# DCN-v2 cross layers on one core: bias load first on ScalarE's queue, bias sums among the fillers, odd lanes' first tail weights on SyncE

## The chip, the cores and the metric

The kernel runs on one core of one Trainium2 chip. The metric is device time in microseconds (us) of one execution; lower is better. The kernel before takes 130.96 us, the median of three runs (130.64 to 131.13).

Times inside a kernel come from traces. They count from the start of the span, which ends with the last instruction and is some 1.9 us shorter than the time measured for the execution. Each trace is one execution. "Landing" is when the last of a load's completion updates arrives at its semaphore.

## The reference

```python
# x0 [4096, 416], ws [6, 416, 416], bs [6, 416], all bf16
def reference(x0, ws, bs):
    x = x0
    for l in range(ws.shape[0]):
        x = x0 * (x @ ws[l] + bs[l]) + x
    return x
```

## The kernel before

The activations are kept transposed: 416 features are three chunks of 128 on the partitions (`x0T_sb`, `xT_sb`) and a tail of 32. The 4096 rows are four superblocks of 1024, so there are 4 x 6 = 24 layer passes. Every matmul of the main part is split over four 32-column tiles of the array ("lanes"). The products of all layers are summed up in the same PSUM banks, since x behind layer l is x0 times (1 + the sum of x W + b over the layers up to l). So the biases are first turned into running sums too, by 16 tiny matmuls against a triangle (`bias_sums`), and these sums enter the layers as scalars.

The start-up matters here. Four queues of work begin at once:

```python
# SyncE's queue
sp.dma_start(xin_sb[:, 0:2, :], x0_v[:, 0:2, :])          # first rows, 208 KB
sp.dma_start(w_sb[:, 0, 0, :], ws[0, 0:128, :])           # first weights (chunk k=0), 104 KB
sp.dma_start(xin_sb[:, 4:6, :], x0_v[:, 4:6, :])          # third rows, 208 KB
sp.dma_start_transpose(x0T_sb[:, :, 768:SB], x0[768:SB, 0:DF])   # the transposing load
...                                                        # layer 1's weights and so on

# ScalarE's queue
act.dma_start(xin_sb[:, 2:4, :], x0_v[:, 2:4, :])         # second rows, 208 KB
act.dma_start(w_sb[:, 0, 1:NC, :], ...)                   # second weights (k=1 and k=2), 208 KB
act.dma_start(xtl_sb[:, :, :], x0_v[:, 6:JS, DF:D])       # tail rows, 16 KB
for g in (1, 3):
    load_wt(act, g, 0, 1, s_wt[0])                        # odd lanes' first tail weights

# GpSimd's queue
pool.memset(ones_sb[:, :], 1.0)
pool.dma_start(bsa_sb[1:L + 1, :], bs[:, :])              # biases, 4.9 KB, 6 rows
...                                                        # identity, triangle, even lanes' tail weights, corner weights
```

(semaphore updates cut). TensorE, meanwhile:

```python
fill(14)                              # 14 groups of four matmuls on constants, to no purpose but time and clock
pe.wait_ge(s_set, 1)                  # identity
for i, (h, c) in enumerate(IN_ORDER): # (0,0),(1,0),(0,1),(1,1),(0,2),(1,2): half h, chunk c
    if i in (0, 1):
        pe.wait_ge(s_xin[h], 16)      # first rows, second rows
    ...                               # two transposes
# first layer pass, first half, chunk by chunk of the contraction
pe.wait_ge(s_w0, 16)
for k in range(NC):
    if k == 1:
        pe.wait_ge(s_w[0], 16)        # second weights
    if k == 2:
        bias_sums()                   # 16 matmuls of six columns
        pe.wait_ge(s_xin[2], 16)      # third rows
        pe.wait_ge(s_xtl0, 16)        # tail rows
        tail_inputs()                 # small transposes of the tails ...
        third_input()                 # ... and of the third quarter
    before_a(k)                       # copies of the transposed chunk k by VectorE or ScalarE
    for m in range(NC):
        step(m, 0, k)                 # "main products" of chunk k
...                                   # then the "row part": tail features and corner weights
```

In these words: the first main products are k = 0 and k = 1, then the small transposes, then k = 2, then the row part. From there the 24 layer passes follow each other.

## Time and profile before

| Quantity (before) | Value | From |
|---|---|---|
| span of the profiled execution | 128.7 us | page |
| TensorE busy | 124.2 us, 97% | page, busy times |
| one layer pass | 4.87 us | chain |
| start of the row part | 8.22 us | TensorE's timeline |
| rest of the span behind it | 120.5 us | difference |
| second weights on ScalarE: issue, landing | 1.35, 5.24 us | trace |
| tail rows on ScalarE: issue, landing | 1.87, 6.17 us | trace |
| third rows on SyncE: issue, landing | 1.82, 5.80 us | trace |
| transposing load on SyncE: issue, landing | 2.29, 7.34 us | trace |

The table is read like this. TensorE is the bound, and everything behind the row part is 120.5 us. Each of the four loads has a place in TensorE's order, and each lands well before TensorE wants it: the second weights at about 5.9 us (3 of the 6 product groups after 5.29), third rows and tail rows at 6.89, the transposing load at 8.8.

### The profile page before, as it was taken

To read this page: it belongs to the slowest core of one execution; us is meant where nothing else is said; L and a number is where in the kernel's file an instruction comes from. 1 tells how busy PE (TensorE), PEld (TensorE's weight loads), DVE (VectorE), ACT (ScalarE), POOL (GpSimd) and SP (SyncE) were. 2 spreads that over 40 slices of the span, in tenths; PEclk is the share of its full clock that TensorE was granted. 3 is DMA by queue.
4 is the path that set the end of the run, shared out by engine and by line. 5 is a ranking of instruction groups with operands and counts; after the bars stand their busy time and mean duration, and the time that the engine had idled before them with its cause. 6 is when DMAs were issued, how large, how long until landed. Compare 5 with 4: busy or idle time off the path is not lost.

```text
span 128.7 us, 5404 instructions
## 1 busy us (share of the span) xinstructions
PE 124.2 (97%) x2448; PEld 62.6 (49%) x2448; DVE 100.1 (78%) x154; ACT 71.3 (55%) x163; POOL 23.1 (18%) x42
## 2 busy tenths in 40 slices
PE   7999999999999999999999999999999999999980
PEld 6654544444444444444445445445445445445450
DVE  2349779779779779779779779779779779789780
ACT  0637357377737357376736456476745555555670
POOL 7802202202202103102102013012012013022130
PEclk9999999999999999999999999999999999999998
DMA  3974399400008698700009996800009900700026
GB/s 109 298 162 104 89 255 174 116 0 5 3 8 167 130 128 185 256 5 0 5 0 175 103 183 140 270 0 0 5 0 95 180 0 0 265 5 5 0 83 190
DMA packets 32918, 12.54 MB, mean 97 GB/s; under 512 B 25338, under 2 KB 32896, under 8 KB 32896
## 3 DMA queue, kind: packets, MB, share of 16 engines
q1 hardware_dynamic: 31488, 11.47, 42.8%
q10 hardware_dynamic: 1184, 0.67, 1.8%
q8 instruction: 19, 0.31, 1.0%
q0 software_dynamic: 224, 0.06, 0.2%
q14 instruction: 3, 0.02, 0.1%
HBM read 2.90 MB, written 3.41 MB: 49 GB/s over the span
## 4 chain that ended last, share of the span: by engine, by line
PE 96%; DVE 1%; DVEq 0%; issue 0%
PE ps L212 84%; PE ps L351 10%; PE ps L250 1%; DVE xo_sb L459 1%; DVE o_sb L464 0%; DVEq L33 0%; PE ps L367 0%
## 5 line engine op out<-in xcount | busy, mean ns | idle before, releaser
L459 DVE SCALAR_TENSOR_TENSOR xT_sb<-ps,cb_sb,x0T_sb 128x512 bf16<-128x512 f32 x120 | 80.9, 744 | 16.5 <-PE ps L351 16.5
L212 PE MATMUL ps<-xT_sb,w_sb 128*32 128x512 bf16 (+1 forms) x1680 | 89.0, 364 | 0.0
L212 PEld LDWEIGHTS ps<-xT_sb,w_sb 128*32 128x32 bf16 x1680 | 43.0, 97 | 38.7 <-issue 4.2
L486 ACT ACTIVATE xt_sb<-xt_sb 32x256 bf16<-32x256 bf16 x80 | 33.1, 414 | 16.6 <-POOL xt_sb L199 15.9
L506 ACT ACTIVATE t_sb<-ps,cb_sb 64x256 f32<-64x256 f32 x48 | 22.5, 469 | 30.1 <-PE ps L212 29.8
L199 POOL TENSOR_TENSOR xt_sb<-t_sb,x0t_sb 128x256 bf16<-128x256 f32 x20 | 13.4, 671 | 83.4 <-ACT t_sb L506 83.4
L212 PE MATMUL ps<-x0T_sb,w_sb 128*32 128x512 bf16 (+1 forms) x336 | 18.5, 364 | 0.0
L459 DVE SCALAR_TENSOR_TENSOR xo_sb<-ps,cb_sb,x0T_sb 128x512 bf16<-128x512 f32 x23 | 15.6, 745 | 3.7 <-PE ps L351 3.3
L212 PEld LDWEIGHTS ps<-x0T_sb,w_sb 128*32 128x32 bf16 x336 | 8.5, 97 | 7.5 <-issue 0.8
L351 PE MATMUL ps<-xt_sb,wt_sb 32*128 32x512 bf16 x80 | 12.1, 379 | 0.0
L519 ACT ACTIVATE x0t_sb<-x_sb 32x256 bf16<-32x256 bf16 x24 | 9.9, 413 | 0.4
L367 PE MATMUL ps<-xt_sb,wt_sb 32*128 32x512 bf16 x40 | 7.8, 385 | 0.0
L351 PE MATMUL ps<-xt_sb,wc_sb 32*128 32x256 bf16 x80 | 7.7, 268 | 0.0
L351 PEld LDWEIGHTS ps<-xt_sb,wt_sb 32*128 32x128 bf16 x80 | 2.3, 92 | 8.5 <-DVE xT_sb L459 8.5
L351 PEld LDWEIGHTS ps<-xt_sb,wc_sb 32*128 32x128 bf16 x80 | 4.0, 93 | 2.3
L199 POOL TENSOR_TENSOR xot_sb<-t_sb,x0t_sb 128x256 bf16<-128x256 f32 x4 | 2.7, 672 | 12.6 <-ACT t_sb L506 12.6
L212 PE MATMUL ps<-const-bfloat16-1.0 128*32 128x256 bf16 x56 | 3.2, 419 | 0.8 <-PEq L557 0.8
L481 ACT ACT_TABLE_LOAD x1 | 1.3, 1283 | 3.6 <-issue 3.6
L432 DVE COPY x0T_sb<-ps 128x256 bf16<-128x256 bf16 x4 | 1.0, 288 | 2.9 <-PE ps L250 2.9
L212 PEld LDWEIGHTS ps<-const-bfloat16-1.0 128*32 128x32 bf16 x56 | 2.4, 144 | 1.2 <-issue 0.8
L351 PE MATMUL ps<-x0t_sb,wt_sb 32*128 32x512 bf16 x16 | 2.5, 380 | 0.0
L168 POOL DMA_DIRECT2D wc_sb<-in_ws_dram x4 | 2.2, 549 | 0.0
(44 smaller groups left out, 28.7 us busy)
## 6 DMA issues: line engine op xcount, KB each, us to landing
out_dram<-o_sb SPq DMA_DIRECT2D x3, 832.0 KB, 4.1
w_sb<-in_ws_dram SPq DMA_DIRECT2D x5, 312.0 KB, 3.9
xin_sb<-in_x_dram SPq DMA_DIRECT2D x2, 208.0 KB, 3.4
out_dram<-o_sb SPq DMA_DIRECT2D x1, 256.0 KB, 2.4
xin_sb<-in_x_dram ACTq DMA_DIRECT2D x1, 208.0 KB, 3.1
w_sb<-in_ws_dram ACTq DMA_DIRECT2D x1, 208.0 KB, 3.9
out_dram<-o_sb SPq DMA_DIRECT2D x1, 208.0 KB, 2.2
out_dram<-o_sb ACTq DMA_DIRECT2D x1, 208.0 KB, 2.7
```

The costliest lines, as they stand in the source:

```text
L168: pool.dma_start(wc_sb[lane(g), a:b, 32 * g:32 * g + 32], ws[a:b, DF:D, DF:D].rearrange("l p n -> p l n")).then_inc(s_wc[i], 16)
L199: pool.tensor_tensor(out=dst, in0=t32_sb[:, n % 2, :], in1=x0t_sb[:, s, 0:G], op=ALU.mult).then_inc(s_xt, 1)
L212: return pe.matmul(dst, lhsT=lhsT, rhs=rhs, start=start, stop=True, skip_group_check=True, tile_position=(0, 32 * q),)
L250: ins = pe.transpose(out=psT[:, IN_BANKS[h][c], (j % 2) * 128:(j % 2 + 1) * 128], in_=xin_sb[:, j, c * 128:(c + 1) * 128], identity=ident[ ...
L351: return pe.matmul(dst, lhsT=lhsT, rhs=srct[lane(g), cols], start=l == 0 and start, stop=True, skip_group_check=True, tile_position=(32 * ...
L367: pe.matmul(ps[:, NC * h + 2, :], lhsT=wt_sb[lane(g), l, 0:128], rhs=srct[lane(g), :].rearrange("p (b r) -> p b r", b=2)[:, ::-1, :], star ...
L432: dve.tensor_copy(out=x0T_sb[:, c, h * 256:(h + 1) * 256], in_=psT[:, IN_BANKS[h][c], 0:256]).then_inc(s_inD, 1)
L459: dve.scalar_tensor_tensor(out=dst, in0=ps[:, NC * half + c, :], scalar=cb_sb[:, c, l:l + 1], in1=x0T_sb[:, c, o:o + H], op0=ALU.add, op1= ...
L481: act.activation(out=x0T_sb[:, 1, h * 256:(h + 1) * 256], in_=psT[:, IN_BANKS[h][1], 0:256], func=ACTF.Copy).then_inc(s_inA, 1)
L486: ins = act.activation(out=buf[lane(g), G:2 * G], in_=buf[lane(g ^ 1), 0:G], func=ACTF.Copy)
L506: ins = act.activation(out=t32_sb[HALVES[h], n % 2, :], in_=tail(h), func=ACTF.Identity, bias=cb_sb[HALVES[h], NC, l:l + 1],)
L519: ins = act.activation(out=x0t_sb[lane(g), s + 1, swap * G:(swap + 1) * G], in_=x4_sb[96:128, s, r * G:(r + 1) * G], func=ACTF.Copy,)
```

## The change

The intent: the bias sums hold TensorE for about 0.3 us between the main products and the small transposes, when it has real work. Put them among the fillers, where TensorE only waits for input. For that the biases have to come sooner, so their load leaves GpSimd's queue and becomes the first on ScalarE's. To make room, the odd lanes' first tail weights leave ScalarE's queue for SyncE's, ahead of the transposing load. The transposes are reordered, first half entirely first, so that the second rows, now second on ScalarE's queue, are wanted later.

```diff
-        IN_ORDER = ((0, 0), (1, 0), (0, 1), (1, 1), (0, 2), (1, 2))
+        IN_ORDER = ((0, 0), (0, 1), (0, 2), (1, 0), (1, 1), (1, 2))
 # SyncE
             sp.dma_start(xin_sb[:, 4:6, :], x0_v[:, 4:6, :]).then_inc(s_xin[2], 16)
+            for g in (1, 3):
+                load_wt(sp, g, 0, 1, s_wt[0])
             sp.dma_start_transpose(x0T_sb[:, :, 768:SB], ...)
 # GpSimd
-            pool.dma_start(bsa_sb[1:L + 1, :], bs[:, :]).then_inc(s_bs, 16)
 # TensorE
-            fill(14)
+            fill(10)
+            bias_sums()
+            fill(2)
...
                             if k == 2:
-                                bias_sums()
                                 pe.wait_ge(s_xin[2], 16)
 # ScalarE
+            act.dma_start(bsa_sb[1:L + 1, :], bs[:, :]).then_inc(s_bs, 16)
             act.dma_start(xin_sb[:, 2:4, :], ...)
             act.dma_start(w_sb[:, 0, 1:NC, :], ...)
             act.dma_start(xtl_sb[:, :, :], ...)
-            for g in (1, 3):
-                load_wt(act, g, 0, 1, s_wt[0])
```

Cut here: the sums go to PSUM bank 1 instead of 4, VectorE copies them before its first input copy, the waits on that copy and on the input copies are renumbered for the new order.

More of the change, by code (lines that the diff above doesn't have):

```diff
@@ L242, in third_input, with bias_sums @@
                     ins.then_inc(s_inT, 1)
-            fill(14)
+            def bias_sums():
+                pe.wait_ge(s_bs, 16)
+                pe.wait_ge(s_zero, 2)
+                pe.wait_ge(s_set, 2)
+                for c in range(NC + 1):
+                    for q in range(4):
+                        f0 = c * 128 + 32 * q if c < NC else DF
+                        ins = tile_mm(ps[lane(q), 1, c * 8:c * 8 + L], bsa_sb[:, f0:f0 + 32], u_sb[:, :], q, True)
+                ins.then_inc(s_cbp, 1)
+            fill(10)
+            bias_sums()
+            fill(2)
             pe.wait_ge(s_set, 1)
             for i, (h, c) in enumerate(IN_ORDER):
-                if i in (0, 1):
+                if c == 0:
                     pe.wait_ge(s_xin[h], 16)
@@ L254, in _ @@
                 ins.then_inc(s_inT, 1)
-            def bias_sums():
-                pe.wait_ge(s_bs, 16)
-                pe.wait_ge(s_zero, 2)
-                pe.wait_ge(s_set, 2)
-                for c in range(NC + 1):
-                    for q in range(4):
-                        f0 = c * 128 + 32 * q if c < NC else DF
-                        ins = tile_mm(ps[lane(q), 4, c * 8:c * 8 + L], bsa_sb[:, f0:f0 + 32], u_sb[:, :], q, True)
-                ins.then_inc(s_cbp, 1)
             def out_chunk(c):
@@ L304, in before_a @@
                         if n == 0:
-                            pe.wait_ge((s_inD, s_inA, s_inD)[k], (2, 2, 4)[k])
+                            pe.wait_ge((s_inD, s_inA, s_inD)[k], (3, 2, 4)[k])
                         else:
@@ L323, in _ @@
                             for m in range(NC):
+                                if k == 0 and m == 1:
+                                    pe.wait_ge(s_cb, 1)
                                 step(m, 0, k)
@@ L334, in _ @@
                         pe.wait_ge(s_te, 1)
-                        pe.wait_ge(s_cb, 1)
                     else:
@@ L428, in _ @@
             dve.memset(bsa_sb[0:1, :], 1.0).then_inc(s_zero, 1)
+            dve.wait_ge(s_cbp, 1)
+            dve.tensor_copy(
+                out=cb_sb[:, :, :], in_=ps[:, 1, 0:8 * (NC + 1)].rearrange("p (c e) -> p c e", e=8)[:, :, 0:L],
+            ).then_inc(s_cb, 1)
             for i, (h, c) in enumerate(IN_ORDER):
@@ L434, in _ @@
                     ).then_inc(s_inD, 1)
-            dve.wait_ge(s_cbp, 1)
-            dve.tensor_copy(
-                out=cb_sb[:, :, :], in_=ps[:, 4, 0:8 * (NC + 1)].rearrange("p (c e) -> p c e", e=8)[:, :, 0:L],
-            ).then_inc(s_cb, 1)
             for c in (0, 2):
@@ L476, in _ @@
             act.dma_start(xtl_sb[:, :, :], x0_v[:, 6:JS, DF:D]).then_inc(s_xtl0, 16)
-            for g in (1, 3):
-                load_wt(act, g, 0, 1, s_wt[0])
             for h in range(2):
-                act.wait_ge(s_inT, h + 3)
+                act.wait_ge(s_inT, NC * h + 2)
                 act.activation(
```

## The prediction

> **What bounds the kernel now.** I read the chain that ended last first, then TensorE's timeline of the first ten microseconds, then the landings of the loads. The chain of the first 14 us (start us, length us, what) is TensorE without a break:
>
> ```profile
> 0.85 3.18 PE ps L212 x51
> 4.03 1.33 PE ps L250 x12
> 5.36 2.93 PE ps L212 x92
> 8.29 0.32 PE ps L351
> ...
> 8.62 0.26 PE ps L351 x4
> 8.88 4.33 PE ps L212 x84
> ```
>
> The page says the same of the whole run:
>
> ```profile
> PE 96%; DVE 1%; DVEq 0%; issue 0%
> ```
>
> The reader should see two things. From 8.88 us on, each layer is one block of 84 matmuls (4.33 us) and a row part; it returns every 4.87 us (8.88, 13.75, 18.62 ...), 24 times, with TensorE never short of input. No line of the change touches this part. Everything that the change can move lies before 8.88 us, and a microsecond counts there only if TensorE's instructions come earlier or later.
>
> TensorE's timeline of that start (start us, length us, shapes, count):
>
> ```profile
> 0.85 3.18 PE L212 MATMUL ps<-const-bfloat16-1.0 128*32 128x256 bf16 x56 [0.85 <-PEq L557]
> 3.96 1.40 PE L250 MATMUL ps<-ident,xin_sb 128*128 128x128 bf16 x12
> 5.29 1.48 PE L212 MATMUL ps<-x0T_sb,w_sb 128*32 128x512 bf16 x24
> 6.70 0.26 PE L212 MATMUL ps<-u_sb,bsa_sb 7*32 7x6 bf16 x16
> 6.89 0.24 PE L212 MATMUL ps<-ident,xin_sb 128*32 128x128 bf16 x3
> ...
> 7.46 0.83 PE L212 MATMUL ps<-x0T_sb,w_sb 128*32 128x512 bf16 x12
> 8.22 0.38 PE L351 MATMUL ps<-x0t_sb,wt_sb 32*128 32x512 bf16 x1
> ...
> 8.48 0.28 PE L351 MATMUL ps<-x0t_sb,wc_sb 32*128 32x256 bf16 x1
> ...
> 8.81 2.45 PE L212 MATMUL ps<-x0T_sb,w_sb 128*32 128x256 bf16 x48
> ```
>
> In order: 14 groups of four fillers; 12 input transposes; the main products for chunks 0 and 1 (24 matmuls, six groups of four); the bias sums; 40 small matmuls that transpose tails and the third quarter (6.89 to 7.46); chunk 2; the row part for the tails; the rest. The bias sums are 16 matmuls of six columns, yet they hold TensorE from about 6.60 (5.29 plus six groups at 0.22; the steady block gives 4.33 us / 19.5 groups of 512 columns = 0.22) to 6.89: **0.29 us**[...]. That is the prize.
>
> **What the skill says.** "TensorE: Matmul & The Clock Gate", section "What's actually happening": the array runs at half rate until it has been busy for a window of about 3.4 us. The trace agrees: a transpose of 128 columns costs 1.33/12 = 0.111 us at 4.0 to 5.3 us, while ten groups of 128 columns cost 0.57/10 = 0.057 us after 6.89. A filler group of 256 columns costs 3.18/14 = 0.227 us with the last one's drain; one filler lasts 0.419, twice 0.21, so without the drain it is (3.18 - 0.2)/14 = 0.213. So the fillers have two purposes: they bridge the wait for the first rows and they earn the full rate, which here arrives around the end of the transposes. "DMA: Bandwidth & Descriptors", section "Issuing engines are not separate DMA queues": loads from several engines share the same 16 DMA engines, and another issuer saves issue time alone. So I take a moved load to shift by issue times and by its place in its queue, not to get bandwidth; the trace has the DMA engines full between about 2 and 8 us (page: busy 9 tenths or more in the second slice, 3.2 to 6.4 us), in agreement. Same page, "Latency and other measured facts": the first byte comes some 0.6 us after issue from SyncE or ScalarE and about 1 us from GpSimd. The trace has no such split but the same order: 2.9 us to landing for the first SyncE load of 208 KB against 3.7 us for 4.9 KB of biases from GpSimd.
>
> **The change part by part.** Landings are issue start plus time to landing, from the view of each load's line.
>
> *Bias load from GpSimd to ScalarE.* Now it is issued at 1.38 and takes 3.7 us: 5.1 us, too late for the fillers.
>
> ```profile
> 1.38 0.72 POOL L165 DMA_DIRECT2D bsa_sb<-in_bs_dram  x1 [0.26 <-issue]
> ...
> 2.56 1.10 POOL L107 DMA_DIRECT2D wt_sb<-in_ws_dram  x2
> 3.67 2.17 POOL L168 DMA_DIRECT2D wc_sb<-in_ws_dram x4
> ```
>
> On ScalarE it is issued at 0.82. A large store at the end of this kernel, with quiet DMA engines, takes 2.2 us; I allow 2.2 to 2.5, an estimate, so it lands at 3.0 to 3.3. GpSimd's queue loses 0.72 us ahead of everything behind it: identity and triangle are ready near 1.9 instead of 2.6, and the first-layer corner weights, whose second load is issued at 4.16 and lands at about 8.4, land at about 7.65. That matters: the second half of the row part starts at 8.48, just behind that landing. Without this step an earlier row part would have been held there and most of the 0.29 us lost.
>
> *Bias sums among the fillers.* TensorE does 10 groups: 0.85 + 10 x 0.213 = 3.0 us. The biases land at 3.0 to 3.3, say 3.15, a wait of about 0.15. The sums cost 0.29 now; with the array at half rate I estimate 0.35. Two more filler groups, 0.43. First transpose: 3.0 + 0.15 + 0.35 + 0.43 = 3.95, against 3.96 now. The rows of the first half land at 0.81 + 2.9 = 3.7, so they don't hold it. Call this shift 0, give or take 0.2.
>
> *New order of the transposes.* Chunk 0 of the second half moves from places 3 and 4 to 7 and 8 of 12. VectorE now begins its first copy 0.43 us after the first transpose (4.39 against 3.96, two transposes in) and copies in 0.29. Six transposes later that becomes 0.43 + 0.64 + 0.29 = 1.36 us, and with about 0.06 for the semaphore the first main matmul comes 1.42 us after the first transpose instead of 1.33: **0.09 us lost**. In return the second rows, now behind the biases on ScalarE's queue (0.5 us per issue: 3.9 becomes about 4.4), are wanted only at 3.95 + 0.64 = 4.6. The wait for the constants' copy before block m=1 is over long before.
>
> *After the main products.* The small transposes follow at once, in the same tiling: **0.29 us saved**. Start: 3.95 + 1.42 + 1.31 = 6.68 instead of 6.89. The tail rows (now 1.87 + 4.3 = 6.2 us) go back by one ScalarE issue less what the queue hides: 6.2 to 6.7. This is the tightest load.
>
> *Odd tail weights on SyncE.* Two issues of about 0.45 us ahead of the transposing load put it from 2.29 to about 3.2; it takes 5.0 us, so 8.2 instead of 7.3. It is wanted at 8.81, in the new kernel at about 8.6: hidden, with 0.4 us to spare. The next weights (3.62 + 4.8 = 8.4, later 9.3) are wanted at 10.9: hidden. ScalarE saves 1.21 us of issues less 0.5 for the biases and loads its table (1.28 us at 3.63) some 0.7 us sooner, so its first copy never has to wait for it; that copy is not on the path.
>
> Sum: 0 (start) + 0.09 - 0.29 = **-0.20 us** on the row part and thus on all after it. With a little given back to the tail rows I predict -0.16: 130.96 - 0.16 = **130.8 us**, 0.1% faster.
>
> **Rivals.**
> *The biases land late.* Each tenth after 3.15 delays the fillers, the transposes and everything else by a tenth; at 3.4 to 3.5 the gain is gone (131.0), at 3.8, where the first 208 KB on this queue land today (0.82 + 3.1 = 3.9), the kernel is 0.4 slower (131.4). For it: the first loads of both queues land at 3.7 and 3.9. Against: those are 208 KB and this is 4.9 KB.
> *The clock.* A hole of 0.2 us and 16 tiny matmuls among the fillers could make the array count as idle for that window and let it run at half rate longer. Between 5.3 and 8.8 us TensorE has about 3.4 us of full-rate work, so a whole missed window would cost up to 1.7 us (132.5). For it: nothing measured, only that the fillers are thinner. Against: the hole is a twentieth of a window. I give it one chance in fifteen.
> *A load takes over the wait.* If the tail rows land near 6.7 or the transposing load near 8.6 TensorE stops there and the whole 0.2 us goes: 131.0.
> *Nothing hidden, better than thought.* If the biases land by 3.0 and the sums cost no more than 0.29 the first transpose comes at 3.75 and the gain is 0.4: 130.55.
>
> **Range and chances.** The three runs of before spread over 0.5 us (130.64 to 131.13), more than the predicted gain. The mechanisms span -0.4 to +0.4 apart from the clock. So 130.45 to 131.25. Two per cent is 2.6 us: no removable time before 8.88 us comes near that, and even a missed clock window stays below. Faster by 2%: 0.01; within: 0.975; slower: 0.015.
>
> **What would show it.** In the changed profile: bias matmuls at 3.0 to 3.3 us; first transpose at 3.8 to 4.1; first main matmul 1.4 us later; the small transposes directly behind the main products near 6.7, with no idle weight load before them; the row part near 8.05; then blocks every 4.87 us as before. I am wrong if TensorE is idle over 0.3 us before the bias sums, if the transposes or the first main groups still run at half rate past 5.5 us, if it waits for tail rows or the transposing load, or if the period of the layers changes.

## The result, and the profile after

The kernel after takes **131.70 us** (median of six runs, 131.51 to 132.28) against 130.78 us (median of six, 130.41 to 131.13) for the kernel before on the same chip in the same rounds. Executions over 1.5% slower than the fastest of the same kernel are left out of the means. The ratio is 1.008, with a 95% interval of 1.0052 to 1.0106. Ratios in this document are the mean time of one kernel's fast runs over that of the other's of the same rounds, so not quite the ratio of the medians that are quoted. So the kernel became 0.8% slower, about 1.0 us; 131.70 lies above the predicted range, which ended at 131.25.

The profiled execution of after has a span of 130.2 us, 1.5 us longer than that of before. The page's summary of the chain that ended last, after (shares of the span by engine):

```profile
PE 90%; DMA 5%; ACTq 1%; DVE 1%; issue 0%; DVEq 0%
```

Where TensorE had 96% of this chain, a DMA now has 5% and ScalarE's issues of DMAs 1%. The chain of the first 15 us of after, in order of time (start us, length us, what), names them:

```profile
0.81 0.58 ACTq L477
...
1.42 0.41 ACTq L478
...
1.86 0.48 ACTq L479
...
2.37 5.93 DMA xtl_sb<-in_x_dram
8.30 0.14 issue
8.43 1.40 PE ps L213 x52
9.83 0.32 PE ps L354
...
10.38 4.33 PE ps L213 x84
```

The start is no longer TensorE without a break. It is ScalarE's queue: bias load (L477), second rows (L478), second weights (L479), then the tail rows, which take 5.93 us for 16 KB. TensorE begins its small transposes at 8.43, behind their landing, and the first block of 84 starts at 10.38 instead of 8.88.

TensorE's timeline of after shows that there is a second wait ahead of that one (start us, length us, shapes, count; in brackets the idle time before it and what ended it):

```profile
0.85 2.32 PE L213 MATMUL ps<-const-bfloat16-1.0 128*32 128x256 bf16 x40 [0.85 <-PEq L559]
3.10 0.27 PE L213 MATMUL ps<-u_sb,bsa_sb 7*32 7x6 bf16 x16
3.30 0.62 PE L213 MATMUL ps<-const-bfloat16-1.0 128*32 128x256 bf16 x8
3.85 0.95 PE L263 MATMUL ps<-ident,xin_sb 128*128 128x128 bf16 x12
5.14 0.83 PE L213 MATMUL ps<-x0T_sb,w_sb 128*32 128x512 bf16 x12 [0.34 <-DVE x0T_sb L439]
7.28 0.83 PE L213 MATMUL ps<-x0T_sb,w_sb 128*32 128x512 bf16 x12 [1.30 <-DMA w_sb<-in_ws_dram]
8.43 0.24 PE L213 MATMUL ps<-ident,xin_sb 128*32 128x128 bf16 x3 [0.33 <-DMA xtl_sb<-in_x_dram]
...
8.99 0.84 PE L213 MATMUL ps<-x0T_sb,w_sb 128*32 128x512 bf16 x12
9.77 0.38 PE L354 MATMUL ps<-x0t_sb,wt_sb 32*128 32x512 bf16 x1
```

Read it down to 5.14 and, in this execution, the change works: the bias sums run among the fillers, the first transpose comes at 3.85 (before: 3.96), the first main product at 5.14 (before: 5.29). Then k = 1 waits for the second weights. The chain does not show this wait, since the tail rows, on the same queue behind those weights, ended later still; a chain names the last wait and not each.

The sum, from starts in the two timelines. A product of three groups takes 0.65 us (half of the 1.31 us that the prediction found for six), so k = 1 could have begun at 5.14 + 0.65 = 5.79 and began at 7.28: 1.49 lost. The small transposes could have begun at 7.28 + 0.65 = 7.93 and began at 8.43: 0.50 lost. The bias sums are gone from this place: 0.29 won. The first main product is 0.15 earlier. 1.49 + 0.50 - 0.29 - 0.15 = 1.55 us, and the row part moved from 8.22 to 9.77, which is 1.55 us. (The brackets say 1.30 and 0.33: they count idle time from the modelled end of the last matmul, which is later than where the next one could start.) The sum says where the time went, not what each load costs by itself: the tail rows landed at 8.30, so the small transposes would have begun near 8.43 even with the second weights on time. The tail rows' landing alone sets the 1.55 us.

Behind the row part nothing changed: 128.75 - 8.22 = 120.53 us in before, 130.23 - 9.77 = 120.46 us in after. The profiled execution of after (132.09 us) happened to be one of its longer ones; on average the loss is 1.0 us.

The loads' own views give the cause a size. Line of the second weights and of the tail rows, before (count; shortest/median/longest issue in ns, first and last issue time; then, as the last line of each load's answer, the time to landing):

```profile
L475 ACTq DMA_DIRECT2D w_sb<-in_ws_dram x1: 492/492/492, 1.3 to 1.3; - x1
...
DMA to landing us min/median/max: 3.9/3.9/3.9
L476 ACTq DMA_DIRECT2D xtl_sb<-in_x_dram x1: 491/491/491, 1.9 to 1.9; - x1
...
DMA to landing us min/median/max: 4.3/4.3/4.3
```

and after:

```profile
L479 ACTq DMA_DIRECT2D w_sb<-in_ws_dram x1: 481/481/481, 1.9 to 1.9; - x1
...
DMA to landing us min/median/max: 5.4/5.4/5.4
L480 ACTq DMA_DIRECT2D xtl_sb<-in_x_dram x1: 492/492/492, 2.4 to 2.4; - x1
...
DMA to landing us min/median/max: 5.9/5.9/5.9
```

Both are issued half a microsecond later, as expected. In before the second weights take 3.9 us from there and the tail rows 4.3 us; in after 5.4 and 5.9. All loads of the start, from the trace (issue → landing, us):

| Load | Queue, before | Before | Queue, after | After |
|---|---|---|---|---|
| first rows | SyncE | 0.81 → 3.68 | SyncE | 0.81 → 3.44 |
| first weights | SyncE | 1.32 → 4.22 | SyncE | 1.32 → 3.76 |
| third rows | SyncE | 1.82 → 5.80 | SyncE | 1.82 → 6.55 |
| transposing load | SyncE | 2.29 → 7.34 | SyncE | 3.26 → 9.27 |
| biases | GpSimd | 1.38 → 5.10 | ScalarE | 0.81 → 2.26 |
| second rows | ScalarE | 0.82 → 3.94 | ScalarE | 1.42 → 4.25 |
| **second weights** | ScalarE | 1.35 → 5.24 | ScalarE | 1.86 → **7.23** |
| **tail rows** | ScalarE | 1.87 → 6.17 | ScalarE | 2.37 → **8.30** |
| odd lanes' tail weights, last | ScalarE | 2.9 → 7.60 | SyncE | 2.80 → 8.24 |
| corner weights of layer 0, last | GpSimd | 4.16 → 8.34 | GpSimd | 3.29 → 8.67 |

For the second weights an issue 0.51 us later made a landing 1.99 us later. That factor of four is what the experiments are about.

A last view, the windows (stretch, its length, busy us and count of TensorE, its weight loads, VectorE, ScalarE, GpSimd; granted clock; DMA share; GB/s). Before:

```profile
5.00:6.25 1.25, 1.25 (x24) 0.68 (x26) 0.49 (x2) 0.59 (x2) 0.84 (x2) 1.00 1.28 256
5.75:6.75 1.00, 1.00 (x28) 0.36 (x23) 0.00 (x0) 0.00 (x0) 0.09 (x1) 1.00 1.18 258
```

After:

```profile
5.00:6.25 1.25, 0.83 (x12) 0.27 (x12) 0.20 (x1) 0.12 (x1) 0.00 (x0) 1.00 1.75 252
5.75:6.75 1.00, 0.22 (x7) 0.00 (x0) 0.00 (x0) 0.00 (x0) 0.00 (x0) 1.00 1.47 130
```

The reader should compare the last two columns. From 5.75 to 6.75 the packets of after fill the DMA engines' time more (share 1.47 against 1.18; above 1 means more than one packet of an engine is open at a time), yet half as many bytes move. The packet records of the trace show why: 17 packets of 256 bytes begin between 5.70 and 6.29 and all end near 6.92 (6.90 to 6.95). In before the longest packet that begins between 5.00 and 6.50 takes 0.28 us (0.44 from 4.25 on). I call them **standing packets**. They have the size of the transposing load's own packets: in before exactly 768 of 256 bytes begin on SyncE's queue by 6.3 us, which is its 256 rows times three chunks of 128 features.

### The profile page after: what moved, and what is told of

It is laid out like the page before. It is cut to its first block, busy times and chain, and to the rows that moved or that the text cites.

```text
span 130.2 us, 5388 instructions
## 1 busy us (share of the span) xinstructions
PE 123.8 (95%) x2440; PEld 61.6 (47%) x2440; DVE 100.0 (77%) x154; ACT 71.4 (55%) x163; POOL 22.6 (17%) x41
## 4 chain that ended last, share of the span: by engine, by line
PE 90%; DMA 5%; ACTq 1%; DVE 1%; issue 0%; DVEq 0%
PE ps L213 80%; PE ps L354 10%; DMA xtl_sb<-in_x_dram 5%; DVE xo_sb L462 1%; DVE o_sb L467 0%; ACTq L477 0%; ACTq L479 0%; ACTq L478 0%; DVEq L33 0%; PE ps L370 0%
## 5 line engine op out<-in xcount | busy, mean ns | idle before, releaser
L444 DVE CAST x0T_sb<-ps 128x256 bf16<-128x256 f32 x2 | 0.8, 420 | 3.8 <-PE ps L213 3.8
L492 ACT ACTIVATE x0t_sb<-ps 128x512 bf16<-128x512 f32 x1 | 0.6, 597 | 3.8 <-PE ps L213 3.8
L213 PEld LDWEIGHTS ps<-const-bfloat16-1.0 128*32 128x32 bf16 x48 | 1.7, 135 | 1.1 <-issue 0.8
```

The lines of the kernel that those rows point to most:

```text
L213: return pe.matmul(dst, lhsT=lhsT, rhs=rhs, start=start, stop=True, skip_group_check=True, tile_position=(0, 32 * q),)
L444: dve.tensor_copy(out=x0T_sb[:, c, 512:768], in_=ps[:, THIRD[c], 0:G]).then_inc(s_inD, 1)
L492: act.activation(out=x0t_sb[:, 0, :], in_=ps[:, 5, :], func=ACTF.Copy).then_inc(s_te, 1)
```

## The experiments

Eighteen runs of fifteen kernels (the kernel after is one of them), in five groups; those of a group ran on the same chip and share the runs of the kernel before. Unless a line says otherwise, "ratio" is against the kernel before. "Weights" is the landing of the second weights (before 5.24, after 7.23), with the issue ahead of it where that matters. Each landing is that of one trace. In the six traces with these weights issued at 1.34 to 1.35 they land between 5.09 and 5.93, in the eight that this document calls late between 6.94 and 7.46; so a difference of a few tenths between two traces shows nothing. The theories that the expectations name:

- **S**: the odd lanes' tail weights, now on SyncE's queue, get in the way of ScalarE's loads.
- **G**: GpSimd's loads, freed of the bias load, come sooner and get in the way.
- **K**: the bias load of six rows runs on six of the 16 DMA engines and disturbs the balance of those behind it. (In after's trace six completion updates of this load come in with its data, at 2.13 to 2.26; loads of 128 rows have 16.)
- **Lateness**: the 0.5 us by which ScalarE's queue starts later is enough by itself, through the place that its loads then take.
- **O** (order): of lateness, what counts is whether the third rows on SyncE's queue come ahead of the second weights.

### Group 1: which part of the change is it?

**Odd lanes' tail weights back on ScalarE** (after, with its second part undone):

```diff
-            for g in (1, 3):
-                load_wt(sp, g, 0, 1, s_wt[0])
 # ScalarE, behind the tail rows
+            for g in (1, 3):
+                load_wt(act, g, 0, 1, s_wt[0])
```

> The changed kernel, with the odd lanes' first tail weights back on ScalarE's queue behind the tail rows, as before. In the changed kernel layer 0's second weights landed at 7.2 us (5.2 before) and the tail rows at 8.3 (6.2 before), and TensorE waited for both. Theory S (the two tail loads on SyncE, and the transposing load that they push back, collide with those two loads): the weights land at about 5.7 again (0.5 later than before, one issue), the row part starts near 8.1, time 130.7. Theory Q (ScalarE's two loads come late because the bias load stands ahead of them): the weights still land near 7 us, time 131.5 to 131.8. Theory G (GpSimd's loads, 0.9 us earlier than before, collide): also 131.5 to 131.8.

Measured: weights 1.86 → 7.26, tail rows 8.65; ratio 1.0006 (0.9942 to 1.0070, three fast runs; the profiled execution was slow at 133.44 us). The weights are as late as in after. That alone fells S as the cause of the late landing. The ratio, with its wide interval, decides nothing. In this trace it is not the weights that TensorE waits for: the second rows land at 6.12 and hold the transposes for 1.49 us, and the full rate comes only at 10.1 us.

**Only the tail weights moved** (before, with just the second part of the change):

```diff
             sp.dma_start(xin_sb[:, 4:6, :], ...)
+            for g in (1, 3):
+                load_wt(sp, g, 0, 1, s_wt[0])
 # ScalarE
-            for g in (1, 3):
-                load_wt(act, g, 0, 1, s_wt[0])
```

> The kernel before with nothing but the odd lanes' first tail weights moved to SyncE ahead of the transposing load. Theory S: this part alone brings the whole loss, weights of layer 0 at about 7 us, time 131.5 to 131.9. Theories Q and G: the weights land at about 5.2 and the tail rows at 6.2 as before, time 130.7 to 131.0.

Measured: ratio 0.9954 (0.9903 to 1.0006); weights 1.34 → 5.93, of which 15 of the 16 engines were done by 4.98; no standing packets. So this part by itself does no harm to the weights or, as far as these runs show, to the time. It does push the tail rows back in the traces: 7.38 here, 6.84 in the repeat below and 6.89 in the run with the bias load last, against 6.17 in before.

**GpSimd's queue held as before** (after, with a bias load nobody reads put back on GpSimd):

```diff
+            pool.dma_start(dum_sb[1:L + 1, :], bs[:, :]).then_inc(s_dum, 16)
```

> The changed kernel with a dummy load of the biases left in the old place of GpSimd's queue (into a tile that nobody reads), so that GpSimd's weight loads are issued from about 2.5 us as before instead of 1.6. Theory G: the weights of layer 0 land at about 5.7 and the time is 130.7, though the corner weights land late again (8.4) and may cost 0.1. Theories S and Q: no change from the changed kernel, 131.5 to 131.8.

Measured: weights 1.88 → 6.94; ratio 1.0033 (0.9968 to 1.0098). Still late: G falls as the cause.

**Tail weights behind the transposing load** (after, two lines of SyncE swapped):

```diff
-            for g in (1, 3):
-                load_wt(sp, g, 0, 1, s_wt[0])
             sp.dma_start_transpose(x0T_sb[:, :, 768:SB], ...)
+            for g in (1, 3):
+                load_wt(sp, g, 0, 1, s_wt[0])
```

> The changed kernel with the two tail loads on SyncE behind the transposing load instead of ahead of it, so that the transposing load is issued at 2.3 us as before. Theory S in its narrow form (it is the transposing load's later issue that collides with layer 0's weights): weights at about 5.7, time 130.7, unless the tail weights themselves come after 8.0 us. Theories Q and G: 131.5 to 131.8.

Measured: weights 1.86 → 7.05; ratio 1.0038 (0.9982 to 1.0095). Late again.

What follows: in all three kernels that keep the bias load first on ScalarE's queue the weights land at 6.9 to 7.3, whatever the tail weights and GpSimd do. It is the bias load's place. The second rows, the first load behind it, are late in these traces too (6.12, 5.25 and 5.43; after 4.25, before 3.94) and hold the transposes for 1.49, 0.62 and 0.81 us. The times of this group are too noisy to say more.

### Group 2: the bias load, or just the half microsecond?

These start from **before** and change only the head of ScalarE's queue.

**A dummy load of six rows first** (the same bytes as the biases, read by nobody; the real bias load stays on GpSimd):

```diff
+            act.dma_start(dum_sb[1:L + 1, :], bs[:, :]).then_inc(s_dum, 16)
             act.dma_start(xin_sb[:, 2:4, :], ...)
```

> The kernel before, with a dummy copy of the 6-row bias load (4.9 KB, nobody reads it) put first on ScalarE's queue; all else as before. The four runs so far: every kernel with the bias load first on ScalarE (changed kernel, a, c, d) has layer 0's second weights at 6.9 to 7.3 us, some DMA engines far behind others, and packets that stand still until 6.5 to 7 us; the one without it (b) has none of this. Theory K (a load of 6 rows runs on 6 of the 16 DMA engines and sets those apart from the rest) and theory Q (everything behind it is one issue later): weights at 6.5 to 7.3 us, time 0.4 to 0.9 over the kernel before. If neither is right (the TensorE program matters): weights at 5.2 to 5.9, time at most 0.3 over.

Measured: ratio 1.0124 (1.0080 to 1.0168); weights 1.86 → 7.46, tail rows 8.82.

**The same bytes as 16 rows**, so that no six engines are singled out:

```diff
+            act.dma_start(dum_sb[:, :], bs.rearrange("l d -> (l d)").rearrange("(p f) -> p f", f=156)).then_inc(s_dum, 16)
```

> As e_dummy6, but the dummy load brings the same 4992 bytes as 16 rows of 156, so that it runs on all 16 DMA engines. Theory K: the spread of the engines goes, weights at 5.5 to 5.9 us, time 0 to 0.3 over the kernel before. Theory Q: as in e_dummy6, weights at 6.5 to 7.3.

Measured: ratio 1.0084 (1.0052 to 1.0115); weights 1.81 → 7.31. As late as with six rows: K falls.

**No load at all, just a wait** of ScalarE for VectorE's first memset:

```diff
         def _(act):
+            act.wait_ge(s_zero, 1)
             act.dma_start(xin_sb[:, 2:4, :], ...)
```

> The kernel before, with no added load; ScalarE merely waits for VectorE's first memset (about 1.45 us) before its first load, so that its loads are issued 0.65 us later, a little more than the 0.6 and 0.5 in the changed kernel. Theory Q (order of arrival of the two queues alone): late weights at 6.5 to 7.3, spread engines, time 0.5 to 1.0 over the kernel before. Theory K: weights at 5.7 to 6.0 with the engines together, and only the direct cost of second rows that land at 4.5 to 4.6 instead of 3.9, 0.3 to 0.5 over.

Measured: ratio 1.0103 (1.0064 to 1.0142), median 132.06 against 130.71 us. ScalarE's timeline of this kernel (start us, length us, line) and its view of DMA issues (KB each, median us from issue to landing):

```profile
1.93 0.49 ACTq L476 DMA_DIRECT2D w_sb<-in_ws_dram  x1
```

```profile
w_sb<-in_ws_dram ACTq DMA_DIRECT2D x1, 208.0 KB, 5.5
```

Nothing was added to the loads, and nothing else was moved; ScalarE's queue starts at 1.47 instead of 0.82, and the weights land at 7.43. **Lateness suffices** for the late landing. The bias load is harmful only by the time that its issue takes. The ratios of these three kernels are no pure price of the late weights: in the order of before the second rows are wanted at 4.15, here they land at 4.75, 4.38 and 4.49, and the first main product comes at 5.56, 5.60 and 5.30 (before 5.29). The windows view has the same signature in this kernel, with few bytes between 5.75 and 6.75:

```profile
5.75:6.75 1.00, 0.38 (x8) 0.00 (x0) 0.00 (x0) 0.56 (x2) 0.09 (x1) 1.00 0.98 92
```

**The bias load last on ScalarE's queue** (before, with the tail weights on SyncE and the bias load behind the tail rows; the sums stay where they were):

```diff
-            pool.dma_start(bsa_sb[1:L + 1, :], bs[:, :]).then_inc(s_bs, 16)
 # ScalarE
             act.dma_start(xtl_sb[:, :, :], ...)
-            for g in (1, 3):
-                load_wt(act, g, 0, 1, s_wt[0])
+            act.dma_start(bsa_sb[1:L + 1, :], bs[:, :]).then_inc(s_bs, 16)
```

(and the tail weights on SyncE as above.)

> The kernel before with the odd tail weights on SyncE ahead of the transposing load (as in b, which was 0.5% faster than before) and the bias load off GpSimd's queue as in the change, but last on ScalarE's queue, behind the tail rows; bias sums stay where they were. Theories K and Q both: nothing big follows the 6-row load on ScalarE's queue, weights at 5.2 to 5.9, time at or below the kernel before (-0.5 to 0).

Measured: ratio 1.0015 (0.9985 to 1.0044); weights 1.35 → 5.58; row part 8.47. Both loads on their new queues, but the weights' place kept: the loss is gone.

### Group 3: what does the lateness run into?

**Third rows behind the tail weights on SyncE** (after, one line moved; the third rows are issued at 2.75 instead of 1.82, so behind the second weights again):

```diff
-            sp.dma_start(xin_sb[:, 4:6, :], x0_v[:, 4:6, :]).then_inc(s_xin[2], 16)
             for g in (1, 3):
                 load_wt(sp, g, 0, 1, s_wt[0])
+            sp.dma_start(xin_sb[:, 4:6, :], x0_v[:, 4:6, :]).then_inc(s_xin[2], 16)
```

> The changed kernel with one pair of lines swapped on SyncE: the two odd tail loads go ahead of the third rows (208 KB) instead of behind them, so that the third rows are issued at about 2.8 us instead of 1.8. Theory O (order across the two queues): in the kernel before, layer 0's second weights are issued at 1.35 on ScalarE and the third rows at 1.82 on SyncE, so the weights go first; in every slow kernel the weights are issued at 1.81 to 1.93, level with the third rows, the two loads share the DMA engines and the transposing load's packets overtake the rest of the weights and stand still. Here the weights are a microsecond ahead again although they are as late as in the changed kernel: expect them at 5.6 to 6.0, third rows by 6.6, row part at 8.0 to 8.4, time 0 to 0.4 us under the kernel before. If the lateness itself is what costs (theory Q without the order), weights still at 6.8 or later and time as the changed kernel, 0.7 to 1.2 over.

Measured: ratio 1.0008 (0.9969 to 1.0047); weights 1.86 → 5.70, tail rows 6.93, third rows 6.72. The profiled execution was a slow one (133.05 us), because the array got its full rate only at 10.4 us; so it was run again:

> i_rows_later once more, because its trace fell in an execution whose array got the full rate only at 10.4 us and says nothing of the row part in an ordinary one. If the gain that was predicted for TensorE's program (0.09 lost, 0.29 saved) is real once layer 0's weights come in time: row part at 8.0 to 8.4 us, small transposes directly behind the main products unless the tail rows (6.9 last time) hold them, time 0 to 0.3 us under the kernel before. If the loads still hold it: row part at 8.4 to 8.8, time level with the kernel before.

Measured (on another chip, in group 4): ratio 1.0050 (1.0005 to 1.0095), runs from 130.70 to 132.65; weights 1.86 → 5.85, tail rows 6.74, third rows 6.94; row part 8.74. The issue view of this run:

```profile
w_sb<-in_ws_dram ACTq DMA_DIRECT2D x1, 208.0 KB, 4.0
```

The issue is as late as in after, at 1.86. With the third rows put behind, the landing is 5.70 and 5.85; 5.24 plus the 0.51 us of later issue is 5.75. So here a later issue costs about itself, and **the surplus of about 1.5 us of after has to do with the third rows' place**. The standing packets shrink with it, to 0.57 and 0.66 us at most. The kernel doesn't become good by it, though: the second rows land at 5.32 (5.00 in the first run) and hold the transposes for 0.69 us,

```profile
5.36 0.51 PE L263 MATMUL ps<-ident,xin_sb 128*128 128x128 bf16 x6 [0.69 <-DMA xin_sb<-in_x_dram]
```

From there on TensorE runs without a wait: the small transposes at 7.42 come 1.30 us behind the first main product at 6.12. The lateness of the second rows is not shown to be a price of the moved line: in a second trace of after itself, below, they land at 5.35.

**Transposing load held** until the second weights and the tail rows have landed (after, with two waits more on SyncE, which also hold back everything behind it on that queue, layer 1's weights first; slower by design, since TensorE then waits for the transposing load, which lands at 10.38):

```diff
+            sp.wait_ge(s_w[0], 16)
+            sp.wait_ge(s_xtl0, 16)
             sp.dma_start_transpose(x0T_sb[:, :, 768:SB], ...)
```

> The changed kernel, but SyncE issues the transposing load only when layer 0's second weights and the tail rows have landed. Asks whether the packets that stand still from 5.5 to about 6.9 us are the transposing load's doing. If they are: no packet over 0.5 us between 5 and 6.5, weights at 5.7 to 6.2, tail rows at 6.2 to 6.8; the time itself is no gain, as the transposing load then lands near 10 and TensorE waits there (0.5 to 1.5 over the kernel before). If they are not: weights again at 6.8 or later.

Measured: ratio 1.0113 (1.0086 to 1.0140); weights 1.86 → 6.81 with 14 of 16 engines by 6.33, tail rows 7.29. No packet of this kernel that begins between 4.25 and 6.25 takes over 0.33 us. That the standing packets go is no surprise, as they have the size of the held load's own. Without them the tail rows come 1.0 us sooner than in after, and below the 7.75 to 8.82 of all eight late traces; the weights come 0.4 us sooner, which is hardly clear of the 6.94 to 7.46 of the others, and 6.81 is far from the 5.75 that the later issue alone would give. So the transposing load, or what stands behind it on SyncE's queue, is a part of the tail rows' surplus; for the weights that is not shown, and it is not the whole.

**Third rows ahead, ScalarE's queue on time** (before, two lines of SyncE swapped: third rows at 1.32, level with the second weights at 1.35, first weights at 1.82):

```diff
-            sp.dma_start(w_sb[:, 0, 0, :], ws[0, 0:128, :]).then_inc(s_w0, 16)
             sp.dma_start(xin_sb[:, 4:6, :], x0_v[:, 4:6, :]).then_inc(s_xin[2], 16)
+            sp.dma_start(w_sb[:, 0, 0, :], ws[0, 0:128, :]).then_inc(s_w0, 16)
```

> The converse on the kernel before: third rows and first weights swapped on SyncE, so the third rows are issued at 1.3, level with layer 0's second weights (1.35) on an untouched ScalarE queue. Theory O: those weights land late though their issue is not late, at 6 us or more with the engines spread, and the time is 0.3 to 1.0 over the kernel before. Theory Q (only a late ScalarE queue costs): weights at 5.2 to 5.5 and at most 0.3 over.

Measured: ratio 1.0091 (1.0046 to 1.0136); weights 1.35 → 5.74, 15 of 16 engines by 5.33; the first weights, now third in the queue, land at 6.11 and hold the first main product until 6.15; no standing packets. The loss in time comes from the first weights and says nothing about O. The landing of the second weights was the test: theory O had asked for 6 us or more. It missed: a level issue alone does not make the surplus. Even the 0.5 us against before lies within the scatter of traces on time (5.09 to 5.93).

**After, once more** beside these:

> The changed kernel again, on the same chip and in the same rounds as i_rows_later: 0.7 to 1.0 over the kernel before, weights of layer 0 at 6.8 to 7.4 us and tail rows at 7.5 to 8.5 in its trace.

Measured: ratio 1.0061 (1.0022 to 1.0101), median 131.51 against 130.98 us; weights 1.87 → 7.09, tail rows 8.25, row part 9.71. The result holds in other rounds. Its start goes another way to the same end, though: here the second rows land at 5.35 instead of 4.25, and after the first six transposes TensorE is idle for 1.08 us until 5.39. The first main product comes at 6.15 instead of 5.14, so the second weights at 7.09 hold it for only 0.33 us (6.15 + 0.65 = 6.80, measured 7.13); then it waits for the tail rows again and begins the small transposes at 8.38 (after: 8.43). Which of the earlier loads holds TensorE differs between executions; the tail rows come last in both.

### Group 4: can the change be had without the lateness?

**Bias load first on SyncE instead** (after; SyncE's queue starts later now, ScalarE's is as early as before, and the transposes begin with the second rows, which ScalarE's queue brings first):

```diff
-        IN_ORDER = ((0, 0), (0, 1), (0, 2), (1, 0), (1, 1), (1, 2))
+        IN_ORDER = ((1, 0), (1, 1), (1, 2), (0, 0), (0, 1), (0, 2))
 # SyncE
+            sp.dma_start(bsa_sb[1:L + 1, :], bs[:, :]).then_inc(s_bs, 16)
             sp.dma_start(xin_sb[:, 0:2, :], ...)
 # ScalarE
-            act.dma_start(bsa_sb[1:L + 1, :], bs[:, :]).then_inc(s_bs, 16)
```

(and ScalarE's two copies in the other order.)

> The changed kernel with the bias load first on SyncE instead of ScalarE, and the second half's input transposes first, since its rows now come first. ScalarE's queue is then as in the kernel before (weights of layer 0 issued at 1.35, third rows on SyncE at 2.4). Theory O: weights at 5.0 to 5.6, no packet over 0.6 us, row part at 8.0 to 8.3, time 0.1 to 0.4 under the kernel before. Theory Q, in the form that any load delayed by the bias load costs: 0.3 or more over.

Measured: ratio 0.9979 (0.9957 to 1.0000), six runs from 130.33 to 130.81 us; weights 1.27 → 4.68, tail rows 5.60, third rows 2.23 → 6.68. TensorE's timeline of it:

```profile
3.86 1.19 PE L264 MATMUL ps<-ident,xin_sb 128*128 128x128 bf16 x12
5.30 1.48 PE L214 MATMUL ps<-x0T_sb,w_sb 128*32 128x512 bf16 x24 [0.25 <-DVE x0T_sb L440]
6.72 0.24 PE L214 MATMUL ps<-ident,xin_sb 128*32 128x128 bf16 x3
```

The main products are one run of 24 again, the small transposes follow at 6.72, with a wait of 0.1 us at most (5.30 + 1.31 = 6.61; the third rows land at 6.68), and the row part starts at 8.06. This is the picture that the prediction drew for after (6.68 and 8.05).

Again, in group 5:

> n_bias_on_sync once more on whatever chip comes, because its first interval (0.9957 to 1.0000) ends at one. If its 0.2 to 0.3 us are real: 0.9965 to 0.9995 again, row part near 8.1 us. If they were scatter: level with the kernel before or above it.

Measured: ratio 0.9997 (0.9981 to 1.0012); weights 4.75, row part 8.12. So the start-up gain of 0.1 to 0.16 us in the traces (8.22 before) isn't clear of the noise in the time.

**Only the tail weights moved, again:**

> b_tails_only (the kernel before with only the odd tail loads moved), 0.5% under the kernel before in 3 rounds with an interval that reaches zero. If that was real: 0.3 to 0.8 us under again. If it was scatter of the loads' landing: within 0.2 us of the kernel before.

Measured: ratio 0.9974 (0.9951 to 0.9997); weights 5.09; row part 8.31. In the trace its row part is not earlier than that of before, so I have no mechanism for the 0.3% and do not call it a gain.

**The transposing load right behind third rows that are level with the weights** (before, with the first weights moved to ScalarE's queue behind the second weights, so that SyncE's queue has third rows at 1.32 and the transposing load at 1.82). This asks whether the transposing load's closeness is the second condition that was missing in the run with the third rows ahead:

```diff
-            sp.dma_start(w_sb[:, 0, 0, :], ws[0, 0:128, :]).then_inc(s_w0, 16)
 # ScalarE, behind the second weights
+            act.dma_start(w_sb[:, 0, 0, :], ws[0, 0:128, :]).then_inc(s_w0, 16)
```

> Why k_rows_sooner (third rows level with layer 0's second weights) brought them only 0.5 us late and no standing packets. There the first weights stood between the third rows and the transposing load. Here, on the kernel before, the first weights go to ScalarE's queue behind the second weights, so third rows (1.3) are level with the second weights (1.35) and the transposing load follows at once (1.8), as in the slow kernels. If the transposing load right behind the level load is the second condition: packets of 0.7 us or more, second weights at 6.3 or later, time 0.8 or more over. If not: second weights at 5.3 to 6.0 and no such packets; the time is then only what the first weights' own lateness costs (0.3 to 0.9).

Measured: weights 1.34 → 5.44, no packet over 0.26 us; ratio 1.0072 (1.0026 to 1.0117), since the first weights land at 6.02 and hold the first product. Not confirmed.

### Group 5: the other queue

**Tail weights back on ScalarE in the kernel with the biases on SyncE**, so that the transposing load follows the third rows closely (2.21 and 2.69):

```diff
 # SyncE
-            for g in (1, 3):
-                load_wt(sp, g, 0, 1, s_wt[0])
 # ScalarE, behind the tail rows
+            for g in (1, 3):
+                load_wt(act, g, 0, 1, s_wt[0])
```

> n_bias_on_sync with the odd tail loads back on ScalarE behind the tail rows: the transposing load is then issued at about 2.7 us instead of 3.7, and comes close behind the third rows (2.2). If the tail part of the change helps on its own account (it was 0.3% under the kernel before when alone): 0.1 to 0.4 us over n_bias_on_sync. If what counts is only that layer 0's weights (1.27) go ahead of the third rows (2.2): level with n_bias_on_sync within 0.15 us, weights at 4.6 to 5.0.

Measured: ratio 1.0011 (0.9992 to 1.0029). The weights are early (1.27 → 4.70), but in the profiled execution the third rows, 2.21 → 7.54, take their place as the late load, with packets of up to 1.09 us at 5.25 to 5.75. TensorE's timeline:

```profile
7.59 0.24 PE L212 MATMUL ps<-ident,xin_sb 128*32 128x128 bf16 x3 [0.78 <-DMA xin_sb<-in_x_dram]
```

So in this trace the same disturbance goes with another load that is still on its way at 5 to 6 us. In that execution (131.12 us) the row part starts at 8.92; four of its six runs took 130.60 to 130.66, so it isn't there every time.

## Why the prediction was wrong

The step that failed is the wait for ScalarE's loads behind the bias load. The prediction had them later by one issue and, with the tail rows at 6.2 to 6.7, in time or a little late. The tail rows landed at 8.30 and 8.25 in the two traces of after, and TensorE stood still for them and for the second weights or second rows ahead of them. By its own steps:

- **Bias load.** It said that the load takes 2.2 to 2.5 us and lands at 3.0 to 3.3. It landed at 2.26, after 1.45 us. The wait of 0.15 us that it allowed did not occur. Right in kind, mis-sized to the good side.
- **Bias sums among the fillers.** Right. Estimated at 0.35 us, they took 0.20 (3.10 to 3.30). First transpose: 3.95 predicted (its terms add up to 3.93), 3.85 measured. Rivals one (late biases) and four fall away with this: the biases were even earlier than in the fourth, and still the kernel lost.
- **Order of the transposes.** 1.42 us from first transpose to first main product predicted, 1.29 measured. That the 0.09 us loss did not appear is luck: in this execution the full rate came at 4.12 us, amid the transposes, and in before at 5.17. In the run with the transposing load held, with the same TensorE program, no wait for rows and the full rate only at 6.88, it took 1.52 us (3.85 to 5.37), so the step was right in kind and at that rate the loss larger, 0.19 us.
- **Second rows.** Said to land at about 4.4, wanted at 4.6. They landed at 4.25 in the first trace, in time, but at 5.35 in the second, where the transposes waited 1.08 us for them. Right only in part of the executions.
- **Corner weights.** Said to land at about 7.65 as GpSimd's queue loses an issue. They were issued sooner (3.29 instead of 4.16) and landed later, 8.67 instead of 8.34. Wrong, without effect here: TensorE came to them after 9.77.
- **Tail rows and what stands before them: the step that failed.** "The tail rows (now 1.87 + 4.3 = 6.2 us) go back by one ScalarE issue less what the queue hides: 6.2 to 6.7." They landed at 8.30. The rule behind it was "So I take a moved load to shift by issue times and by its place in its queue". The first half of it was applied, the second was not carried over to the *other* queue: the weights' place against SyncE's third rows. And the second weights, on the same queue and wanted first of all, were not worked out at all. By the rule they would have landed at 5.24 + 0.51 = 5.75, against a want at 3.95 + 1.42 + 0.65 = 6.02: enough on paper, by 0.27 us. They landed at 7.23. So it is the rule that failed, and not just its use. For the tail rows it gives 6.17 + 0.50 = 6.67 and is 1.6 us short.
- **Transposing load.** 8.2 predicted, 9.27 measured, wanted near 10.3 by then: hidden, as said.
- **Third rival**, a load that takes over the wait: right in kind. It named the tail rows, and missed the second weights. Its size, "the whole 0.2 us goes", was far too small: the two waits were 1.49 + 0.50 = 1.99 us. A wait that takes a gain's place is not bounded by the gain.
- **Clock rival.** Not in after's trace: full rate from 4.12 us, before from 5.17. It did show in other executions of kernels with holes in TensorE's start-up, at 9.5 to 10.4 us in four traces (tail weights back on ScalarE, GpSimd's queue held, the first run with the third rows behind, and the transposing load behind level third rows), where it adds to the loss.
- **The layers.** Untouched, as said: 120.5 us behind the row part in both.
- **-0.20 us.** The row part at 8.05 was reached (8.06, 8.12) when the biases went to the head of SyncE's queue with the transposes begun by the second rows. So the sum was right for a kernel that keeps ScalarE's loads in place; the time then moved by -0.2% and 0.0%.

What is shown: the loss is the row part's later start (1.55 and 1.49 us in the two traces of after); it is waits for ScalarE's loads, the tail rows last and, ahead of them, the second weights in one trace and mostly the second rows in the other; the half microsecond at the head of ScalarE's queue produces the late landings, with any load or none (three kernels, ratios 1.008 to 1.012); and putting the third rows behind brings the weights' landing back to about what the later issue costs (5.70 and 5.85).

What is only partly shown: the part of the transposing load. Holding it, and the loads behind it on its queue, brings the tail rows from 8.30 to 7.29 and the weights from 7.23 to 6.81, the latter hardly clear of the scatter. In seven of the eight traces of kernels with late weights, other than the one with the transposing load held, the DMA share between 5.00 and 6.25 us is 1.48 to 1.85 (the one with just a wait on ScalarE has 1.35); in the others it is at most 1.33, apart from the last experiment (1.67), which has another late load.

What stays open: why the second rows are late in some executions and not in others; why neither a level issue alone, nor that with the transposing load right behind, makes the surplus where ScalarE's queue is on time; and what the standing packets stand for. The packet records show when a packet began and ended, not what it waited for. No kernel here beats the kernel before beyond doubt: the two candidates gave 0.9979 and 0.9997, and 0.9954 and 0.9974.

## What to carry to other kernels

An issue that costs half a microsecond at the head of a queue moves every load behind it, and where several queues fill the DMA engines the landing can move by several times that: here by four times, and no longer so once a load of another queue was put behind. Before putting something first, list *every* load behind it with its landing and the time at which it is wanted, beside the other queues' issue times at that point; a margin of a few tenths of a microsecond counted as none here (0.27 us on paper, missed by over a microsecond). And put what you add at the head of the queue whose next loads have the slack.

## What the Trainium skill lacked or had wrong

- "DMA: Bandwidth & Descriptors", section "Issuing engines are not separate DMA queues", says that another issuing engine saves issue time alone and that loads interleave. It lacks, as do the other pages, a figure for what a late issue can cost a load that way: with ScalarE's queue 0.6 us later and nothing else changed, a 208 KB load landed 2.2 us later (5.24 to 7.43); with another queue's 208 KB load put behind, as little as 0.5 us (5.70 with the issue 0.51 us later).
- The same page, section "Rules for kernel authors", says that a transposing load beside ordinary loads needs nothing. That is about correctness, and all results here were correct. It lacks a cost in time: with one under way, packets of 256 bytes stood for up to 1.2 us in after (17 of them ended together near 6.92), and holding it and the loads behind it brought the tail rows from 8.30 to 7.29 us. In before, with the same load under way, none did.
- The same page, section "Anatomy of one DMA — SWDGE (gpsimd) path", gives a fixed cost of about 2.0 us for a load from GpSimd. Here 4.9 KB took 3.7 us from GpSimd among the other loads of the start (1.38 to 5.10), so that formula falls short there. The same bytes as the first load of ScalarE's queue, another path, took 1.45 us.
- "TensorE: Matmul & The Clock Gate", section "What's actually happening", lets the moment of full rate vary by 500 ns. The fillers begin at 0.85 us in all traces here, yet 14 of the 20 have the full rate between 3.5 and 5.8 us, a spread of 2.3 us; two have it at 6.1 and 6.9, and four, all of kernels with holes in TensorE's start-up, at 9.5 to 10.4 us.
